# Eight PSUM banks as one pool instead of four pools, in a block-sparse attention and feed-forward kernel

## The chip, the cores and the metric

The kernel runs on one core of a Trainium2 chip. The metric is the device time of one execution in microseconds (us), the median of several runs; lower is better. The core has five engines that run their own instruction streams in order: the matrix engine (PE, whose weight loads are listed apart as PEld), the vector engine (DVE), the scalar engine (ACT), GpSimd (POOL) and the engine that only issues transfers (SP). PE writes its products into PSUM, an accumulation memory of eight banks, each 2 KB in each of 128 partitions; one product tile of 128x512 fp32 fills a bank. DVE and ACT read the banks and write to SBUF, the main on-chip memory.

## The reference

Four batches, eight heads, 768 positions, head size 64. Positions are grouped in 24 blocks of 32. A query block attends to itself and its two neighbours, to the first and the last block, and to three sampled blocks; the first and last query blocks attend to everything. The heads' outputs, side by side, are the input of a feed-forward layer with a swish that has a factor for each hidden column.

```python
scores = scale * np.matmul(q, k.transpose(0, 1, 3, 2))
mask = np.abs(blk_i - blk_j) <= window
mask = mask | (blk_i == 0) | (blk_j == 0) | (blk_i == n_blocks - 1) | (blk_j == n_blocks - 1)
for qb in range(n_blocks):
    for kb in sampled_blocks[qb]:
        mask[qb * block:(qb + 1) * block, kb * block:(kb + 1) * block] = True
scores = np.where(mask, scores, -1000000000.0)
scores = scores - np.max(scores, axis=-1, keepdims=True)
attn = np.exp(scores)
attn = attn / (np.sum(attn, axis=-1, keepdims=True) + 1e-09)
...
x = np.ascontiguousarray(attn_out.transpose(0, 2, 1, 3)).reshape(B * S, H * D)
...
h = x @ w_in
g = h * (1.0 / (1.0 + np.exp(-beta * h)))
return (g @ w_out).astype(np.float32)
```

`attn_out` is attn times v; x has 3072 rows of 512, h 2048 columns, and the result is 3072 x 512.

## The kernel before

**Attention.** Work goes in chunks of 128 query positions (4 blocks) of one batch, and each chunk in two quads Q of four heads: 4 x 6 x 2 = 48 steps. For each batch q, k and v are loaded and cast to fp16 (POOL after the start); q and k are transposed on PE into `qT` and `kT` (`transpose_pair`, PSUM tiles tp_q and tp_k, L209). `gather_chunk` copies the keys of each query block side by side into `KG` (ACT L250, POOL L255 and L261); the values come by DMA from a table in DRAM into `VA` and `VB` (`gather_v`, three buffers each).

One step consists of

- `scores`: 16 small products per pair of heads into two PSUM tiles sc (L321); DVE takes the negated maximum nm of each (L328) and ACT writes the exponentials probs (L331);
- `probs_T`: eight PE transposes of probs into one PSUM tile tp_p (L342), copied by DVE to probsT (L346);
- `attend`: products of probsT with VA and VB into one PSUM tile av (L393, and L405 for the global rows), whose last column is the row sum; DVE divides (L411, L412) and writes x16.

The rows of the first and last blocks are done once per batch and head pair in `global_scores` (two PSUM tiles scg, L358, read by DVE gnm L366 and twice by ACT gp L371) and `global_T` (PSUM tile tp_g, L380, copied by DVE to gpT, L383). When both quads of a chunk are done, `x_transpose` turns x16 on PE (tile tp_x, L435) into xT (DVE L437).

**Feed-forward.** Chunks are put together in groups of 2, 2, 4, 4, 4, 4, 4. For each group there are 16 units `h_unit`: four matmuls into a PSUM tile hps (L449), ACT tanh into t_sb (L453), DVE (t+1)*h into g (L455). For each chunk there are two half units `o_unit`: eight matmuls each into one PSUM tile ops (L466), which is held from the first half to the end of the second, then scaled by ACT into osb (L472) and stored. The units wait in a queue `moe_q` and `run_moe` deals them out between the attention pieces of the steps, to a plan by due times.

**Order.** `tc.manual_schedule(engines={ET.PE, ET.Pool, ET.SP})` keeps the instructions of PE, POOL and SP in the order in which the program traces them. DVE and ACT are ordered by a scheduler at build time. All engines run in order; semaphores are set by the framework. A tile of a PSUM pool with N buffers is given one of N banks, and its first matmul waits until the tile that had the bank before has been read for the last time.

**PSUM.** Four pools share the eight banks:

```python
sc_psum = ctx.enter_context(tc.tile_pool(name="sc_psum", bufs=2, space=bass.MemoryType.PSUM))
tp_psum = ctx.enter_context(tc.tile_pool(name="tp_psum", bufs=2, space=bass.MemoryType.PSUM))
av_psum = ctx.enter_context(tc.tile_pool(name="av_psum", bufs=1, space=bass.MemoryType.PSUM))
mm_psum = ctx.enter_context(tc.tile_pool(name="mm_psum", bufs=3, space=bass.MemoryType.PSUM))
```

sc and scg take the two banks of the first, all transposes (tp_k, tp_q, tp_p, tp_g, tp_x) the two of the second, av the one of the third, hps and ops the three of the last.

Of the kernel before, what the change touches and what calls it, by code (L numbers as in the profile page):

```python
# [10 lines left out]
FP32 = mybir.dt.float32  # L11
FP16 = mybir.dt.float16
# [8 lines left out]
def kernel(  # L21
# [43 lines left out]
    o_pool = ctx.enter_context(tc.tile_pool(name="osb", bufs=2))  # L65
    g_pool = ctx.enter_context(tc.tile_pool(name="gbuf", bufs=2))

    sc_psum = ctx.enter_context(tc.tile_pool(name="sc_psum", bufs=2, space=bass.MemoryType.PSUM))
    tp_psum = ctx.enter_context(tc.tile_pool(name="tp_psum", bufs=2, space=bass.MemoryType.PSUM))
    av_psum = ctx.enter_context(tc.tile_pool(name="av_psum", bufs=1, space=bass.MemoryType.PSUM))  # L70
    mm_psum = ctx.enter_context(tc.tile_pool(name="mm_psum", bufs=3, space=bass.MemoryType.PSUM))


    sb_handle = dataclasses.replace(sampled_blocks.tensor, shape=[NB, 6], dtype=I32)
# [129 lines left out]
    def transpose_pair(name, b, Q, pr):  # L204
        h16 = halves[(name, b, Q)]
        dstT = (qT if name == "q" else kT)[b]
        tp = tp_psum.tile([P, 1024], FP16, tag="tp", name=f"tp_{name}")
        for e in range(6):
            nc.tensor.transpose(out=tp[:, e * P:(e + 1) * P],  # L209
                                in_=h16[:, e, 2 * pr:2 * pr + 2, :].rearrange(  # L210
                                    "p h d -> p (h d)"),
                                identity=identity)
        return nc.scalar.activation(
            out=dstT[:, 2 * Q + pr, :].rearrange("p (s e) -> p s e", e=6),
            func=AF.Copy, scale=SCALE if name == "q" else 1.0,
            in_=tp[:, 0:S].rearrange("p (e s) -> p s e", e=6))
# [88 lines left out]
    def scores(b, c, Q, KG):  # L305
        scs = []
        for hp in range(2):
            sct = sc_psum.tile([P, 2, 256], FP32, tag="sc", name="sc")
            scs.append(sct)

        for hp in range(2):
            for pr in range(2):
                pg = 2 * Q + pr
                for j in range(4):
                    i = 4 * c + j
                    rr = slice(64 * hp, 64 * hp + 64)
                    if 0 < i < NB - 1:
                        rhs = KG[rr, j, pg, :]
                    else:
                        rhs = kT[b][rr, pg, 0:256]  # L320
                    nc.tensor.matmul(scs[hp][BLK * j:BLK * (j + 1), pr, :],  # L321
                                     lhsT=qT[b][rr, pg, i * BLK:(i + 1) * BLK],
                                     rhs=rhs, start=True, stop=True,
                                     tile_position=(64 * hp, BLK * j))
        pt = p_pool.tile([P, 4, 256], FP16, tag="probs", name="probs")
        nm = small_pool.tile([P, 2, 2], FP32, tag="nm", name="nm")
        for hp in range(2):
            nc.vector.tensor_reduce(out=nm[:, hp, :], in_=scs[hp], axis=AX.X, op=ALU.max,  # L328
                                    negate=True)
            for pr in range(2):  # L330
                last_exp[0] = nc.scalar.activation(  # L331
                    out=pt[:, 2 * pr + hp, :], in_=scs[hp][:, pr, :],
                    func=AF.Exp, bias=nm[:, hp, pr:pr + 1], scale=1.0)
        return pt
# [1 line left out]
    last_exp = [None]  # L336

    def probs_T(pt):
        tp = tp_psum.tile([P, 1024], FP16, tag="tp", name="tp_p")
        for u in range(4):  # L340
            for half in range(2):
                nc.tensor.transpose(out=tp[:, u * 256 + half * P:u * 256 + (half + 1) * P],  # L342
                                    in_=pt[:, u, half * P:(half + 1) * P],
                                    identity=identity)
        ptT = pt_pool.tile([P, 4, 2, P], FP16, tag="probsT", name="probsT")
        nc.vector.tensor_copy(out=ptT.rearrange("p u h q -> p (u h q)"), in_=tp)  # L346
        return ptT

    def global_scores(b, Q, hp):
        rr = slice(64 * hp, 64 * hp + 64)  # L350
        halves = []
        for s in range(2):
            sct = sc_psum.tile([P, 2, 256], FP32, tag="sc", name="scg")
            sct = sct.rearrange("p a w -> p (a w)")[:, 0:384]
            halves.append(sct)
            for j in range(4):
                pr, blk = j // 2, (j % 2) * (NB - 1)
                nc.tensor.matmul(sct[BLK * j:BLK * (j + 1), :],  # L358
                                 lhsT=qT[b][rr, 2 * Q + pr, blk * BLK:(blk + 1) * BLK],
                                 rhs=kT[b][rr, 2 * Q + pr, 384 * s:384 * (s + 1)],  # L360
                                 start=True, stop=True,
                                 tile_position=(64 * hp, BLK * j))
        nm = small_pool.tile([P, 4], FP32, tag="gnm", name="gnm")
        pg = gp_pool.tile([P, S], FP16, tag="gp", name="gp")
        for s in range(2):
            nc.vector.tensor_reduce(out=nm[:, s:s + 1], in_=halves[s],  # L366
                                    axis=AX.X, op=ALU.max, negate=True)
        nc.vector.tensor_reduce(out=nm[:, 2:3], in_=nm[:, 0:2], axis=AX.X, op=ALU.min)  # L368
        pv = pg.rearrange("p (e s) -> p e s", e=6)
        for s in range(2):  # L370
            nc.scalar.activation(  # L371
                out=pv[:, :, 64 * s:64 * (s + 1)],
                in_=halves[s].rearrange("p (s e) -> p e s", e=6),
                func=AF.Exp, bias=nm[:, 2:3], scale=1.0)
        return pg

    def global_T(pg):
        tp = tp_psum.tile([P, 1024], FP16, tag="tp", name="tp_g")
        for ct in range(6):
            nc.tensor.transpose(out=tp[:, ct * P:(ct + 1) * P],  # L380
                                in_=pg[:, ct * P:(ct + 1) * P], identity=identity)
        gT = gpt_pool.tile([P, 6, P], FP16, tag="gpT", name="gpT")
        nc.vector.tensor_copy(out=gT.rearrange("p c q -> p (c q)"), in_=tp[:, 0:S])  # L383
        return gT

    def attend(b, c, Q, ptT, VA, VB, gTs, x16):
        av = av_psum.tile([P, 4, VW], FP32, tag="av", name="av")
        js = [j for j in range(4) if 0 < 4 * c + j < NB - 1]
        for u in range(4):
            h = 4 * Q + u  # L390
            for half, V in ((0, VA), (1, VB)):
                for j in js:
                    nc.tensor.matmul(av[BLK * j:BLK * (j + 1), u, :],  # L393
                                     lhsT=ptT[:, u, half, BLK * j:BLK * (j + 1)],
                                     rhs=V[:, j, h * VW:(h + 1) * VW],
                                     start=(half == 0), stop=(half == 1),
                                     tile_position=(0, BLK * j))
        if len(js) < 4:
            j = 0 if c == 0 else 3
            bi = 0 if c == 0 else 1  # L400
            for u in range(4):
                pr, hp = u // 2, u % 2
                jj = 2 * pr + bi
                for ct in range(6):
                    nc.tensor.matmul(av[BLK * j:BLK * (j + 1), u, :],  # L405
                                     lhsT=gTs[hp][:, ct, BLK * jj:BLK * (jj + 1)],
                                     rhs=v16[b][:, ct, 4 * Q + u, :],
                                     start=(ct == 0), stop=(ct == 5),
                                     tile_position=(0, BLK * j))
        rec = small_pool.tile([P, 4], FP32, tag="rec", name="rec")  # L410
        nc.vector.reciprocal(out=rec, in_=av[:, :, D])  # L411
        nc.vector.tensor_tensor(out=x16[:, 4 * Q:4 * Q + 4, :], in0=av[:, :, 0:D],  # L412
                                in1=rec[:, :].to_broadcast([P, 4, D]), op=ALU.mult)
# [14 lines left out]
    def x_transpose(b, c, x16):  # L428
        gi, s = slot_of[(b, c)]
        if s == 0:  # L430
            xT_tiles[gi] = x_pool.tile([P, N_DMC, 512], FP16, tag="xT", name="xT")
        tp = tp_psum.tile([P, 1024], FP16, tag="tp", name="tp_x")
        xf = x16.rearrange("p h d -> p (h d)")
        for cc in range(N_DMC):
            nc.tensor.transpose(out=tp[:, cc * P:(cc + 1) * P],  # L435
# [7 lines left out]
    def h_unit(gi, f):  # L443
        n = P * len(groups[gi])
        if f == 0:
            g_tiles[gi] = g_pool.tile([P, N_FFC, 512], FP16, tag="g", name="g")
        hp = mm_psum.tile([P, 512], FP32, tag="mm", name="hps")
        for cc in range(N_DMC):
            nc.tensor.matmul(hp[:, 0:n], lhsT=w_in_sb[:, cc, f * P:(f + 1) * P],  # L449
                             rhs=xT_tiles[gi][:, cc, 0:n],  # L450
# [9 lines left out]

    def o_unit(gi, s, part):
        if part == 0:
            o_live[(gi, s)] = mm_psum.tile([P, D_MODEL], FP32, tag="mm", name="ops")
        op = o_live[(gi, s)]
        for f in range(8 * part, 8 * part + 8):
            nc.tensor.matmul(op, lhsT=g_tiles[gi][:, f, s * P:(s + 1) * P],  # L466
# [305 lines left out]
```

## Time and profile before

| | |
|---|---|
| time, median of three runs | 355.84 us (352.66 to 357.5) |
| profiled execution | 355.98 us |
| its span, first to last instruction | 354.1 us |
| mean granted PE clock | 0.96 of full |
| costliest lines of PE | L449 hps 101.2 us, L466 ops 89.9 us, L342 tp_p 33.5 us, L321 sc 29.3 us |
| costliest lines of DVE | L455 g 67.3 us, L328 nm 62.9 us, L346 probsT 32.5 us |
| costliest lines of ACT | L331 probs 76.8 us, L453 t_sb 69.6 us, L250 KG 34.0 us |

All times come from one profiled execution. Busy time counts an engine's instructions and not its waits; a wait is listed with the instruction that ended it. A page's slices divide the span into 40 parts of 8.9 us, and a digit is the busy share in tenths. A line such as `PE sc L321 <- ACT gp L371: 12.3, 10, 1.9` reads: PE, before an instruction of line 321 that writes sc, stood idle until ACT's instruction of line 371 that writes gp was done; 12.3 us in total, 10 times, the longest 1.9 us. In the timeline each row has its start, its length, and in brackets the idle time before it and what ended that.

### The profile page before, as it was taken

The page shows a single profiled execution, that of the slowest core. Times are in us where ns is not written, and L with a number is a line of the kernel's source. Part 1 is how long each engine was busy: PE and PEld are TensorE (multiplying, and loading weights), DVE is VectorE, ACT ScalarE, POOL GpSimd, SP SyncE. Part 2 cuts the span into 40 slices and gives each one's busy share as a digit, 9 for nine tenths or more (in the row PEclk, how much of TensorE's full clock was granted, in tenths as well). Part 3 has the DMA queues.
Part 4 walks back from the last instruction along what each step waited for, and adds up shares of the span by engine and source line. Part 5 has one row for each costly group of instructions (what it writes and reads, how often), then busy time and mean ns, then how long its engine had stood idle before and what let it go on. Part 6 is the DMA issues. An engine that isn't in the chain of part 4 may idle for free.

```text
span 354.1 us, 11302 instructions
## 1 busy us (share of the span) xinstructions
PE 299.5 (85%) x4288; PEld 168.8 (48%) x4288; DVE 227.1 (64%) x506; ACT 230.2 (65%) x447; POOL 174.3 (49%) x451
## 2 busy tenths in 40 slices
PE   0565877769687899986999999997889999899995
PEld 0343535646445565543545665453435655444442
DVE  3667766748778566678687668677777666543400
ACT  2687466988766888677678887666656664354421
POOL 5659939599957864955556819725015100000000
PEclk9999988989987889999899999999999999999999
DMA  7979999998887853655878617724036150000012
GB/s 182 380 202 223 225 323 314 291 227 184 200 291 226 246 149 84 169 138 142 254 221 245 168 35 190 184 69 103 33 88 156 43 141 31 31 30 31 31 71 79
DMA packets 40135, 56.95 MB, mean 161 GB/s; under 512 B 7280, under 2 KB 31984, under 8 KB 40080
## 3 DMA queue, kind: packets, MB, share of 16 engines
q0 software_dynamic: 10160, 26.21, 28.2%
q1 hardware_dynamic: 24400, 23.71, 25.5%
q10 hardware_dynamic: 5520, 6.30, 5.3%
q8 instruction: 34, 0.56, 0.7%
q14 instruction: 21, 0.17, 0.2%
HBM read 50.77 MB, written 9.62 MB: 171 GB/s over the span
## 4 chain that ended last, share of the span: by engine, by line
PE 56%; DVE 13%; ACT 13%; issue 5%; DMA 4%; POOL 2%; POOLq 0%; ACTq 0%; DVEq 0%; SPq 0%
PE ops L466 20%; PE hps L449 18%; ACT probs L331 5%; PE tp_p L342 5%; DVE g L455 4%; DMA VB<-vtab 4%; PE sc L321 3%; ACT gp L371 3%; DVE nm L328 3%; PE av L393 3%; ACT t_sb L453 3%; DVE gnm L366 2%; PE av L405 2%; ACT KG L250 2%; PE scg L358 1%
## 5 line engine op out<-in xcount | busy, mean ns | idle before, releaser
L449 PE MATMUL hps<-xT,w_in_sb 128*128 128x512 f16 (+1 forms) x448 | 101.2, 361 | 5.5 <-DVE g L455 4.9
L455 DVE SCALAR_TENSOR_TENSOR g<-t_sb,hps 128x512 f16<-128x512 f16 (+1 forms) x112 | 67.3, 609 | 49.5 <-ACT t_sb L453 48.3
L453 ACT ACTIVATE t_sb<-hps,beta_h_sb 128x512 f16<-128x512 f32 (+1 forms) x112 | 69.6, 634 | 39.2 <-PE hps L449 38.5
L466 PE MATMUL ops<-w_out_sb,g 128*128 128x512 f16 x384 | 89.9, 381 | 0.0
L331 ACT ACTIVATE probs<-sc,nm 128x256 f16<-128x256 f32 x192 | 76.8, 476 | 19.5 <-DVE nm L328 19.2
L328 DVE TENSOR_REDUCE nm<-sc 128x2 f32<-128x512 f32 x96 | 62.9, 686 | 26.7 <-PE sc L321 26.6
L280 POOL DMA_INDIRECT VB<-vtab,idx_b x40 | 38.9, 972 | 81.9 <-PE av L393 64.3
L261 POOL COPY KG<-kT 128x128 f16 (+1 forms) x264 | 63.2, 293 | 4.4 <-PE sc L321 4.0
L449 PEld LDWEIGHTS <-w_in_sb 128*128 128x128 f16 x448 | 43.0, 102 | 39.3 <-issue 9.2
L466 PEld LDWEIGHTS <-g 128*128 128x128 f16 x384 | 36.7, 98 | 43.2 <-issue 2.8
L321 PE MATMUL sc<-KG,qT 64*32 64x256 f16 x704 | 29.3, 292 | 13.7 <-ACT gp L371 9.0
L250 ACT COPY KG<-kT 128x768 f16<-128x768 f16 (+1 forms) x44 | 34.0, 782 | 6.5 <-PE sc L321 5.9
L342 PE MATMUL tp_p<-identity,probs 128*128 128x128 f16 x384 | 33.5, 236 | 1.2 <-issue 1.2
L346 DVE COPY probsT<-tp_p 128x1024 f16<-128x1024 f16 x48 | 32.5, 677 | 1.3 <-PE tp_p L342 1.1
L472 ACT ACTIVATE osb<-ops 128x512 f32<-128x512 f32 x24 | 14.4, 599 | 23.9 <-PE ops L466 23.9
L371 ACT ACTIVATE gp<-scg,gnm 128x384 f16<-128x384 f32 x32 | 16.8, 577 | 17.8 <-DVE gnm L368 13.3
L342 PEld LDWEIGHTS <-probs 128*128 128x128 f16 x384 | 24.2, 105 | 5.5 <-issue 3.1
L321 PEld LDWEIGHTS <-qT 64*32 64x32 f16 x768 | 9.6, 92 | 35.4 <-issue 24.0
L209 PE MATMUL tp_k<-identity,k 128*128 128x128 f16 x96 | 9.8, 252 | 14.2 <-ACT k L202 12.0
L393 PEld LDWEIGHTS <-probsT 128*32 128x32 f16 x1408 | 15.5, 99 | 12.4 <-issue 9.1
L412 DVE TENSOR_TENSOR x<-av,rec 128x256 f16<-128x256 f32 x48 | 20.2, 422 | 1.2
L393 PE MATMUL av<-VA,probsT 128*32 128x65 f16 x704 | 20.1, 201 | 0.9 <-DVE x L412 0.8
(69 smaller groups left out, 299.4 us busy)
## 6 DMA issues: line engine op xcount, KB each, us to landing
VA<-vtab SPq DMA_DIRECT2D x16, 390.0 KB
out_dram<-osb ACTq DMA_DIRECT2D x24, 256.0 KB
VB<-vtab SPq DMA_DIRECT2D x147, 32.5 KB
st_k<-in_k_dram POOLq DMA_DIRECT2D x6, 768.0 KB, 5.9
st_v<-in_v_dram POOLq DMA_DIRECT2D x6, 768.0 KB, 8.5
st_q<-in_q_dram POOLq DMA_DIRECT2D x6, 768.0 KB, 6.4
VA<-vtab SPq DMA_DIRECT2D x8, 292.5 KB
vtab<-v POOLq DMA_DIRECT2D x3, 780.0 KB, 7.1
```

Of the source, the lines that this page charges most:

```text
L250: (nc.scalar.copy if steady else nc.vector.tensor_copy)(out=KG[:, j0:j1, w0:w0 + 2, 0:96], in_=dataclasses.replace(base, ap=[ap[0], [BLK, ...
L261: eng.tensor_copy(out=KG[:, j, p0:p1, 128 + BLK * r:160 + BLK * r], in_=kv[:, p0:p1, bass.ds(k_regs[(4 * c + j, r)] * BLK, BLK)])
L280: nc.gpsimd.indirect_dma_start(VB[:, j, :], None, tab[:, :], bass.IndirectOffsetOnAxis(idx_b[:, 4 * c + j:4 * c + j + 1], 0))
L321: nc.tensor.matmul(scs[hp][BLK * j:BLK * (j + 1), pr, :], lhsT=qT[b][rr, pg, i * BLK:(i + 1) * BLK], rhs=rhs, start=True, stop=True, tile_ ...
L328: nc.vector.tensor_reduce(out=nm[:, hp, :], in_=scs[hp], axis=AX.X, op=ALU.max, negate=True)
L331: last_exp[0] = nc.scalar.activation(out=pt[:, 2 * pr + hp, :], in_=scs[hp][:, pr, :], func=AF.Exp, bias=nm[:, hp, pr:pr + 1], scale=1.0)
L342: nc.tensor.transpose(out=tp[:, u * 256 + half * P:u * 256 + (half + 1) * P], in_=pt[:, u, half * P:(half + 1) * P], identity=identity)
L393: nc.tensor.matmul(av[BLK * j:BLK * (j + 1), u, :], lhsT=ptT[:, u, half, BLK * j:BLK * (j + 1)], rhs=V[:, j, h * VW:(h + 1) * VW], start=( ...
L449: nc.tensor.matmul(hp[:, 0:n], lhsT=w_in_sb[:, cc, f * P:(f + 1) * P], rhs=xT_tiles[gi][:, cc, 0:n], start=(cc == 0), stop=(cc == N_DMC - 1))
L453: nc.scalar.activation(out=t_sb[:, 0:n], in_=hp[:, 0:n], func=AF.Tanh, bias=0.0, scale=beta_h_sb[:, f:f + 1])
L455: nc.vector.scalar_tensor_tensor(out=g_tiles[gi][:, f, 0:n], in0=t_sb[:, 0:n], scalar=1.0, in1=hp[:, 0:n], op0=ALU.add, op1=ALU.mult)
L466: nc.tensor.matmul(op, lhsT=g_tiles[gi][:, f, s * P:(s + 1) * P], rhs=w_out_sb[:, f, :], start=(f == 0), stop=(f == N_FFC - 1))
```

## The change

The four pools become one of eight banks, and every PSUM tile of the kernel is taken from it under one tag. Each tile is declared as a whole bank and then viewed in its former shape. No instruction is added or removed, and the traced order of the program stays.

```diff
-    sc_psum = ctx.enter_context(tc.tile_pool(name="sc_psum", bufs=2, space=bass.MemoryType.PSUM))
-    tp_psum = ctx.enter_context(tc.tile_pool(name="tp_psum", bufs=2, space=bass.MemoryType.PSUM))
-    av_psum = ctx.enter_context(tc.tile_pool(name="av_psum", bufs=1, space=bass.MemoryType.PSUM))
-    mm_psum = ctx.enter_context(tc.tile_pool(name="mm_psum", bufs=3, space=bass.MemoryType.PSUM))
+    ring = ctx.enter_context(tc.tile_pool(name="ring", bufs=8, space=bass.MemoryType.PSUM))
@@ transpose_pair; probs_T, global_T and x_transpose likewise
-        tp = tp_psum.tile([P, 1024], FP16, tag="tp", name=f"tp_{name}")
+        tp = ring.tile([P, 1024], FP16, tag="bank", name=f"tp_{name}")
@@ scores
-            sct = sc_psum.tile([P, 2, 256], FP32, tag="sc", name="sc")
+            sct = ring.tile([P, 512], FP32, tag="bank", name="sc").rearrange(
+                "p (a w) -> p a w", a=2)
@@ global_scores
-            sct = sc_psum.tile([P, 2, 256], FP32, tag="sc", name="scg")
-            sct = sct.rearrange("p a w -> p (a w)")[:, 0:384]
+            sct = ring.tile([P, 512], FP32, tag="bank", name="scg")[:, 0:384]
@@ attend
-        av = av_psum.tile([P, 4, VW], FP32, tag="av", name="av")
+        av = ring.tile([P, 512], FP32, tag="bank", name="av")[:, 0:4 * VW].rearrange(
+            "p (u e) -> p u e", e=VW)
@@ h_unit
-        hp = mm_psum.tile([P, 512], FP32, tag="mm", name="hps")
+        hp = ring.tile([P, 512], FP32, tag="bank", name="hps")
@@ o_unit
-            o_live[(gi, s)] = mm_psum.tile([P, D_MODEL], FP32, tag="mm", name="ops")
+            o_live[(gi, s)] = ring.tile([P, D_MODEL], FP32, tag="bank", name="ops")
```

More of the change, by code (lines that the diff above doesn't have):

```diff
@@ L338, in probs_T @@
     def probs_T(pt):
-        tp = tp_psum.tile([P, 1024], FP16, tag="tp", name="tp_p")
+        tp = ring.tile([P, 1024], FP16, tag="bank", name="tp_p")
         for u in range(4):
@@ L377, in global_T @@
     def global_T(pg):
-        tp = tp_psum.tile([P, 1024], FP16, tag="tp", name="tp_g")
+        tp = ring.tile([P, 1024], FP16, tag="bank", name="tp_g")
         for ct in range(6):
@@ L431, in x_transpose @@
             xT_tiles[gi] = x_pool.tile([P, N_DMC, 512], FP16, tag="xT", name="xT")
-        tp = tp_psum.tile([P, 1024], FP16, tag="tp", name="tp_x")
+        tp = ring.tile([P, 1024], FP16, tag="bank", name="tp_x")
         xf = x16.rearrange("p h d -> p (h d)")
```

## The prediction

> **What bounds the kernel now.** I read the page first: busy time, slices, chain of waits. Bounds of 2% (about what a measurement of this kernel can tell from no change) lie at 348.7 and 363.0 us around the median of 355.84.
>
> ```profile
> PE 299.5 (85%) x4288; PEld 168.8 (48%) x4288; DVE 227.1 (64%) x506; ACT 230.2 (65%) x447; POOL 174.3 (49%) x451
> ...
> PE   0565877769687899986999999997889999899995
> ...
> PEclk9999988989987889999899999999999999999999
> DMA  7979999998887853655878617724036150000012
> ...
> PE 56%; DVE 13%; ACT 13%; issue 5%; DMA 4%; POOL 2%; POOLq 0%; ACTq 0%; DVEq 0%; SPq 0%
> ```
>
> PE is the busiest engine and carries over half of the chain. It is idle for 54.6 us of 354.1; 16.0 of these fall before 28 us (loads, first casts), 3.7 after 310. The rest, some 35 us, is what a PSUM change can touch. The waits of the PE alone, from 28 us on, say who ended them:
>
> ```profile
> PE sc L321 <- ACT gp L371: 12.3, 10, 1.9
> PE hps L449 <- DVE g L455: 4.9, 4, 2.1
> PE scg L358 <- ACT probs L331: 3.0, 5, 0.8
> ...
> PE tp_k L209 <- DVE probsT L346: 2.2, 2, 1.3
> PE sc L321 <- ACT probs L331: 1.8, 1, 1.8
> ```
>
> (waiter, releaser, us in total, times, longest). None of these is a wait for data: a score product doesn't read gp, nor hps the g of the unit before. The releaser is the last reader of the bank that the waiter is about to overwrite. The timeline shows one such wait:
>
> ```profile
> 96.34 0.39 PE L435 MATMUL tp_x<-identity,x 128*128 128x128 f16 x4
> ...
> 97.63 1.05 ACT L371 ACTIVATE gp<-scg,gnm 128x384 f16<-128x384 f32 x2 [0.61 <-DVE gnm L368]
> 98.27 0.87 PE L321 MATMUL sc<-KG,qT 64*32 64x256 f16 x16 [1.53 <-ACT gp L371]
> ```
>
> PE ends tp_x at 96.73, then stands until ACT's first gp exponential has left a bank of the two-bank score pool; its KG had been ready for 9.7 us. I went through all 432 PSUM tiles this way, setting the first matmul of each against the end of the last reader of the tile before it in the same bank. 48 tiles after 28 us begin 0.05 us after that end, and the PE idle time before them is 29.0 us: 10.4 up to 84, 4.2 in 84-110, 4.3 in 110-150, 4.7 in 150-190, 0.2 in 190-230, 5.2 in 230-270, none later.
>
> **What the change moves.** It adds and removes no engine operation. In the built program the orders of PE, POOL and SP (with all DMA issues) are the same row for row; DVE and ACT are ordered by the scheduler, and 58 of 506 DVE rows and 62 of 446 ACT rows stand elsewhere, mostly one place away. The banks do not rotate strictly: of 424 reuses 177 come eight tiles later, 101 seven, 65 nine, 39 six; the nearest is four and the farthest 28, where an ops tile is held (up to 17.8 us).
>
> Are the new banks free in time? With the times of before, of all 424 reuses only one would come too early (scg at 107.7, by 0.18 us); the next tightest has 0.56 us left, nine have under 1 us, the median 3.2.
>
> **Term 1, waits after 84 us: 14.0 gained.** The ceiling is their 18.6 us. For a floor I leave all other engines where they are, and let each wait shrink only as far as the tightest data edge of the next 6 us allows (start of a matmul less the end of what it reads). That returns 3.3 of 4.2 in 84-110, 2.6 of 4.3, 4.1 of 4.7, 0.2 of 0.2 and 4.9 of 5.2: 15.2. The next waits are then those with the small margins: tp_p for probs (0.75 us at 219.7), tp_x for x16 (0.65 at 268.0), tp_k for POOL's cast (nothing at 115.6 and 186.8). Against it stand new bank waits: 0.2 us with the old times, 3.3 us (8 tiles) if PE always led its readers by 1 us, about the mean of the waits removed. I take 1.2, so 14.0; range 11.9 to 18.6. PE is in order, so behind such a wait all PE work queues, and DVE and ACT behind that.
>
> **Term 2, the clock: 2.5 gained.** PE's granted clock by stretch (PE busy, clock, DMA share, GB/s):
>
> ```profile
> 100.30:103.70 3.40, 3.40 (x23) 0.50 0.62 232
> 110.50:117.30 6.80, 6.05 (x86) 0.50 0.88 281
> 124.20:127.60 3.40, 3.40 (x74) 0.50 1.10 320
> 168.60:172.00 3.40, 3.40 (x19) 0.51 1.03 343
> ...
> 190.00:230.00 40.00, 39.49 (x627) 1.00 0.60 162
> ```
>
> Each slow stretch follows bank waits by a few us (96.7-98.3, 108.4-111.3, 121.1-123.7, 163.7-167.4). In one, the four hps matmuls of a unit take 1.71 us, against 0.86 elsewhere. 17.0 us at half clock cost up to 8.5 us; 240-270 has as many waits and no slow stretch, so the link is loose: I take under a third.
> The Trainium skill speaks against the change here (TensorE: Matmul & The Clock Gate, A second HAM failure mode: psum-queue depth-cycling): it tells of a kernel that cycled through PSUM banks each iteration, idled briefly between groups and so swung between half and full clock. By that rule the rate of 84-172 (five windows of 3.4 us in 88 us) would go on over 172-310, an estimate of 8 windows at 1.7 us, and the sum would be 356 instead of 340. Row 190:230, where three banks are cycled at clock 1.00, does not show it.
>
> **Term 3, waits before 84 us: 2.5 gained.** 10.4 us of bank waits, and a floor by data edges of 6.8, but others pace this stretch:
>
> ```profile
> 28.00:84.00 56.00, 41.16 (x818) 28.53 (x819) 38.54 (x92) 42.17 (x89) 45.40 (x114) 0.91 1.13 267
> ```
>
> (busy PE, PEld, DVE, ACT, POOL, clock, DMA share, GB/s). The DMA engines are over full, POOL is busy for 45.4 of 56 and hands PE the K and q casts and the KG gather of the second batch just in time. POOL itself waits for PE only once, 3.0 us for av L393 at 69.5. So 0 to 6.8; 2.5, near that row.
>
> **Term 4, the new DVE and ACT order: 2.5 lost.** A row moved ahead of one that was ready earlier delays it by a row's length (0.41 to 0.69 us). Taking each DVE row's input time from the old trace, rows stood behind a later-ready one for 22 us in total in the old order (after 40 us) and for 32 us in the new; ACT's went from 4 to 6. Of those 12 us the chain share of DVE and ACT, 26%, gives about 3; PE's earlier start hides some: 2.5, range 10 lost to 2.5 gained (the scheduler planned the new order for free banks). DVE is idle 36%; without that cover all 12 us would show.
>
> **Term 5, semaphores: 0.5 lost.** PE gets 15 more separate semaphore instructions (86 for 71); the trace has such a one at 51 ns: 0 to 0.8.
>
> Sum: 14.0 + 2.5 + 2.5 - 2.5 - 0.5 = 16.0. The profiled execution took 355.98 us (span 354.1 and 1.9 around it), 0.14 over the median: 355.98 - 16.0 = 340.0.
>
> **Rivals.**
> *The waits come back as data waits* (chance 0.16). For it: from 147 to 165 and 237 to 266 us the chain runs through DVE and ACT pieces (g, nm, probs, gp), and DVE is busy 16.4 of 20 us in 150-170. If these pace, only 110-150 (2.6) and 190-230 (0.2) come back, with the clock's 2.5 less terms 4 and 5: 2.3 gained, 353.7. Against: in those stretches DVE itself waits for sc and ACT, which a bank-blocked PE delivers late.
> *Slower: one late reader stops every kind of work* (0.10). Before, a late score reader blocked scores only; now the bank may be hps's or tp's. From 28 to 310 us a tile starts every 0.7 us, so eight tiles pass in 5.6 us; the longest holds are sc 5.0 and scg 4.5 us. If the new DVE/ACT order lengthens the hold of a score pair past that in each of the 36 steps from 84 us on, by 0.8 us, it costs 29 us: 340 + 29 = 369. It is slower by 2% from 0.64 us a step. Against: the moves of order are one place.
> *More than forecast* (0.06): all 18.6 us and all slow stretches (8.5) go, with term 3 and no losses: 29.6, so 326.4.
> *That the change doesn't do what it says*, a pool of eight in name only, is excluded by the bank list.
>
> The forecast has 0.68, its own range 330 to 348. Faster: 0.68 + 0.06 = 0.74; same 0.16; slower 0.10. The range 329 to 353 leaves out the fourth case, the slower one and a little of the second.
>
> **What would show it.** Right: in the waits of PE the rows sc <- gp, scg <- probs and hps <- g shrink from 20 us to under 5; PE idle in 84-270 falls from 19 to under 7 us; the end of the score products, now 293.7 us, comes some 15 us earlier; clock 0.50 stretches after 84 are fewer than five. Wrong: sc still waits for an ACT reader (the third case); tp_p, tp_g, tp_x wait for probs, gp, x16 for over 10 us (the second); before 84 us the gain exceeds 5 us (term 3); the clock falls below 1.00 after 172 us.

## The result, and the profile after

The changed kernel takes 339.04 us (median of 4 runs, 338.19 to 341.58), the kernel before 356.1 us beside it: a ratio of 0.9545, 95% interval 0.9494 to 0.9596. Ratios and their intervals, here and below, leave out runs more than 1.5% over the fastest of their kernel; medians are of all runs. The forecast was 340.0. The profiled execution took 339.05 us, its span 337.3.

The waits of PE alone in the changed kernel, from 28 us on (waiter, releaser, us in total, times, longest; lines 320 and 321, for instance, are the same statement, as the diff shifts the numbers):

```profile
PE tp_g L378 <- ACT gp L369: 6.7, 9, 2.2
PE tp_k L207 <- POOL k L200: 6.7, 2, 6.4
PE tp_x L434 <- DVE x L411: 4.2, 6, 1.4
PE tp_q L207 <- POOL q L200: 2.8, 2, 2.4
PE tp_p L341 <- issue: 2.2, 1, 2.2
```

The three rows of before are gone: sc no longer waits for gp, scg not for probs, and hps for g is 0.5 us. What is left are waits for data: tp_g reads gp, tp_k and tp_q the cast k and q, tp_x the x16. Matched tile by tile as in the prediction, the bank waits after 28 us fell from 29.1 to 1.5 us, and PE's other waits, nearly all for data, rose from 6.0 to 25.5 us. PE's idle time fell by only 7.1 us (54.6 to 47.5), but the span by 16.8. The other 9.7 us are busy time. The page's first line, its clock and the group of the score products:

```profile
PE 289.8 (86%) x4288; PEld 163.6 (49%) x4288; DVE 223.2 (66%) x506; ACT 226.7 (67%) x447; POOL 174.8 (52%) x451
...
PEclk9996997779997699998999999999999999999999
...
L320 PE MATMUL sc<-KG,qT 64*32 64x256 f16 x704 | 24.7, 291 | 6.2 <-DVE KG L259 3.2
```

and the same group in the kernel before:

```profile
L321 PE MATMUL sc<-KG,qT 64*32 64x256 f16 x704 | 29.3, 292 | 13.7 <-ACT gp L371 9.0
```

PE is busy for 9.7 us less with the same 4288 matmuls, 4.6 of them in the score products: these are busy for 24.7 us and were for 29.3, while one takes 291 ns and took 292. So they are not shorter, they lie closer together. The timeline of before showed the 16 products of a step (16 for all four heads, eight in each of the two sc tiles) at 98.27 lasting 0.87 us. The same step (the 16th) in the changed kernel:

```profile
91.15 0.39 PE L434 MATMUL tp_x<-identity,x 128*128 128x128 f16 x4
91.47 0.42 PE L320 MATMUL sc<-KG,qT 64*32 64x256 f16 x16
91.82 0.21 PE L392 MATMUL av<-VA,probsT 128*32 128x65 f16 x4
```

No wait stands before them, and the 16 last 0.42 us: the eight of one tile and the eight of the other, which use different row halves of the array, run at once. In the kernel before, the second tile's bank was released by the second gp exponential, 0.5 us after the first, and as PE was then working on the first tile, this second wait appears as busy time. In 13 of 45 steps after 28 us the second score tile began over 0.3 us after the first, and those pairs took 0.93 us on average against 0.45; after the change it is 1 of 44.

Stage by stage, from the 13th step (first of the second batch) to the 48th, in the changed kernel (window, length, busy PE, PEld, DVE, ACT, POOL, granted clock, DMA share, GB/s):

```profile
79.00:105.00 26.00, 23.12 (x463) 14.32 (x462) 23.31 (x59) 21.83 (x52) 20.10 (x51) 1.00 0.82 216
105.00:117.00 12.00, 5.76 (x42) 2.81 (x48) 2.31 (x7) 4.18 (x8) 10.13 (x25) 0.57 0.97 299
117.00:145.70 28.70, 28.70 (x530) 17.69 (x521) 22.49 (x46) 25.44 (x50) 20.33 (x54) 1.00 0.59 157
145.70:180.40 34.70, 32.98 (x502) 17.00 (x501) 28.41 (x61) 27.16 (x55) 25.03 (x60) 0.95 0.77 221
180.40:212.10 31.70, 31.42 (x539) 18.90 (x538) 22.85 (x45) 26.05 (x50) 20.40 (x54) 1.00 0.55 154
212.10:248.20 36.10, 35.51 (x507) 17.29 (x506) 28.57 (x60) 26.03 (x52) 12.21 (x36) 1.00 0.41 106
```

PE is 95 to 100% busy from 117 us on. The second line is a stall that the kernel before did not have: PE stands from 104.8 to 111.2 us before tp_k, until POOL has cast the third batch's keys, and its clock falls to half for 10.2 us around it. POOL in the changed kernel, then the same cast in the kernel before:

```profile
99.53 1.88 POOL L223 CAST v<-st_v 128x384 f16<-128x384 f32 x4 [4.06 <-DMA st_v<-in_v_dram]
110.23 1.85 POOL L200 CAST k<-st_k 128x384 f16<-128x384 f32 x4
```

```profile
114.22 1.85 POOL L202 CAST k<-st_k 128x384 f16<-128x384 f32 x4
```

PE is at tp_k 10.6 us earlier than before (104.8 against 115.4 us), the cast only 4.0 us earlier; POOL had itself stood for the load of v. The lead over the kernel before grows 4.0 us up to the 13th step, 7.7 at the 17th, falls to 6.0 at the 21st, after the stall, and then grows to 17.0 at the 45th.

### The profile page after: what moved, and what is told of

Its sections match the earlier page's. It is cut to its first block, busy times and chain, and to the rows that moved or that the text cites. A ratio compares the mean times of both kernels' runs of the same rounds, so it can differ in the third digit from the quotient of the medians.

```text
span 337.3 us, 11313 instructions
## 1 busy us (share of the span) xinstructions
PE 289.8 (86%) x4288; PEld 163.6 (49%) x4288; DVE 223.2 (66%) x506; ACT 226.7 (67%) x447; POOL 174.8 (52%) x451
## 3 DMA queue, kind: packets, MB, share of 16 engines
q0 software_dynamic: 10160, 26.21, 29.1%
## 4 chain that ended last, share of the span: by engine, by line
PE 59%; DVE 10%; ACT 8%; DMA 8%; issue 6%; POOL 6%; SPq 1%; POOLq 1%; DVEq 0%; ACTq 0%
PE ops L465 20%; PE hps L448 19%; PE tp_p L341 4%; DMA st_kq<-in_k_dram 4%; PE av L392 3%; PE sc L320 3%; DVE g L454 3%; ACT probs L330 3%; PE av L404 3%; DMA VA<-vtab 3%; DVE nm L327 2%; POOL KG L259 2%; ACT gp L369 2%; DVE gnm L364 2%; PE tp_k L207 2%
## 5 line engine op out<-in xcount | busy, mean ns | idle before, releaser
L448 PE MATMUL hps<-xT,w_in_sb 128*128 128x512 f16 (+1 forms) x448 | 98.7, 356 | 1.0 <-DVE xT L436 0.5
L465 PE MATMUL ops<-w_out_sb,g 128*128 128x512 f16 x384 | 90.9, 384 | 0.0
L448 PEld LDWEIGHTS <-w_in_sb 128*128 128x128 f16 x448 | 42.1, 100 | 34.0 <-issue 2.8
L341 PE MATMUL tp_p<-identity,probs 128*128 128x128 f16 x384 | 31.9, 229 | 2.8 <-issue 2.2
L320 PE MATMUL sc<-KG,qT 64*32 64x256 f16 x704 | 24.7, 291 | 6.2 <-DVE KG L259 3.2
L341 PEld LDWEIGHTS <-probs 128*128 128x128 f16 x384 | 23.2, 102 | 6.8 <-issue 3.7
L364 DVE TENSOR_REDUCE gnm<-scg 128x1 f32<-128x384 f32 x32 | 16.7, 550 | 8.6 <-PE scg L356 8.6
L392 PEld LDWEIGHTS <-probsT 128*32 128x32 f16 x1408 | 16.2, 99 | 11.8 <-issue 9.2
```

Source lines behind the costliest of these rows:

```text
L320: nc.tensor.matmul(scs[hp][BLK * j:BLK * (j + 1), pr, :], lhsT=qT[b][rr, pg, i * BLK:(i + 1) * BLK], rhs=rhs, start=True, stop=True, tile_ ...
L392: nc.tensor.matmul(av[BLK * j:BLK * (j + 1), u, :], lhsT=ptT[:, u, half, BLK * j:BLK * (j + 1)], rhs=V[:, j, h * VW:(h + 1) * VW], start=( ...
```

## The experiments

Theory A: the gain is the removed bank waits; a product finds a bank as soon as any is free. Rival B: the gain came from the new DVE and ACT order (the scheduler's). Rival C: the number of banks for a kind of product counts, sharing does little. In each run the kernel before is measured on the same chip.

**The same order on all engines, two bank plans.** Both kernels get, from step 4 on, the traced order on DVE and ACT as well:

```diff
+        if n == 4:
+            ctx.enter_context(tc.manual_schedule(
+                engines={ET.PE, ET.Pool, ET.SP, ET.DVE, ET.Activation}))
```

Four pools (e1):

> The four pools of before; from step 4 on DVE and ACT also keep the traced order (112 of 534 DVE and 109 of 474 ACT instructions move against before). Theory A (the gain is the bank waits): the bank waits stay, 25 to 35 us after 28 us, time 350 to 365. Rival B (the gain came from the new order that the scheduler found for DVE and ACT): nothing is said of this one alone, it is the base for e2.

One pool (e2):

> The pool of eight, with DVE and ACT in the same traced order as e1: all five engines have the same instructions in the same order in e1 and e2, so only the banks differ. Theory A: 13 to 20 us faster than e1, bank waits after 28 us under 4 us. Rival B: within 5 us of e1.

Measured: 385.7 us with four pools (ratio to before 1.0837, 1.0798 to 1.0875) and 357.07 with one (1.0033, 0.9997 to 1.0069): 28.6 us apart, more than theory A said, and the first one far above its range. Bank waits after 28 us are 47.6 and 15.0 us, where 25 to 35 and under 4 were expected. The longest waits of PE with four pools, then with one:

```profile
PE sc L321 <- ACT gp L371: 20.4, 12, 3.6
PE hps L449 <- DVE g L455: 8.8, 4, 3.4
```

```profile
PE tp_g L378 <- ACT gp L369: 7.0, 6, 2.0
PE tp_x L434 <- DVE x L411: 3.4, 6, 1.5
```

The banks alone make this difference, since nothing else differs; B falls as the cause of the gain as a whole. In the change itself the order of DVE and ACT moved too, and what that added or cost within the 17.1 us was not measured by itself. The size was off in part because more products were bank-blocked in the traced order (58 tiles over 47.6 us; 48 over 29.1 before). The clock differs too: its mean was 0.911 with four pools and 0.962 with one, and how much of the 28.6 us goes through it is not told apart. Order is not nothing: the traced one costs 30 us with four pools, and puts the one-pool kernel 18 us over the changed kernel.

**Fewer banks in one pool.**

```diff
-    ring = ctx.enter_context(tc.tile_pool(name="ring", bufs=8, space=bass.MemoryType.PSUM))
+    ring = ctx.enter_context(tc.tile_pool(name="ring", bufs=7, space=bass.MemoryType.PSUM))
```

> One pool of seven banks, the eighth unused; orders of DVE and ACT as in the changed kernel but for one instruction. Theory A (banks free in time because every product can take any free one): set against the recorded times of the changed kernel, 51 tiles would come too early, by 15 us in all, but against the times of before only 3; so some waits return: 341 to 346. Rival B: 338 to 340, as the order is the same. Rival C (the number of banks is what counts, sharing does little): over 347.

And with `bufs=6`:

> One pool of six banks, two unused. Theory A: 23 tiles come too early even with the times of before (7 us), so 344 to 352, still not slower than the four pools with eight banks. Rival C: over 356, since six banks are fewer than eight. Rival B: 338 to 341.

Measured: 342.48 us (0.9636, 0.9602 to 0.9669) with seven, 343.83 us (0.9659, 0.9610 to 0.9707) with six, just under its range. Bank waits after 28 us are 4.0 and 9.2 us. Six shared banks beat eight divided ones by 12 us; C falls, and both times are above what B said for them. The waits of PE with six banks:

```profile
PE tp_k L207 <- POOL k L200: 5.7, 2, 3.6
PE tp_q L207 <- POOL q L200: 5.1, 1, 5.1
PE tp_x L434 <- DVE x L411: 2.5, 4, 1.3
```

Data waits head the list here too: going from six to eight banks removes bank waits of 7.7 us, but brings 4.8 us to the end.

**Sharing in part.** Scores and feed-forward products in one pool of five, transposes and av as before; then scores, transposes and av in one pool of five, feed-forward as before:

```diff
+    ring = ctx.enter_context(tc.tile_pool(name="ring", bufs=5, space=bass.MemoryType.PSUM))
+    tp_psum = ctx.enter_context(tc.tile_pool(name="tp_psum", bufs=2, space=bass.MemoryType.PSUM))
+    av_psum = ctx.enter_context(tc.tile_pool(name="av_psum", bufs=1, space=bass.MemoryType.PSUM))
```

The first (e5):

> Scores and feed-forward products share five banks; the transposes keep their two, av its one. Theory A: the waits of sc and scg for each other and of hps for hps go (24 of the 29 us of before), those of the transposes stay (4.5 us): 341 to 346. Rival B (order): 31 ACT and 26 DVE instructions move against before, so no clear figure; equal to e6 only by chance.

The second (e6):

> Scores, transposes and av share five banks; feed-forward products keep their three. Theory A: sc, scg, transposes and av stop waiting (24 of 29 us), hps still waits for hps (5 us before, up to 7): 341 to 347.

Measured: 344.02 us (0.9682, 0.9606 to 0.9758) and 344.46 us (0.9628, 0.9534 to 0.9723), both in range. Either way of freeing the scores brings some 12 of the 17 us, though more bank waits are left than the 4.5 and the 5 to 7 us that were expected: 12.0 and 13.0 us.

**A third score bank, taken from the feed-forward.**

```diff
-    sc_psum = ctx.enter_context(tc.tile_pool(name="sc_psum", bufs=2, space=bass.MemoryType.PSUM))
+    sc_psum = ctx.enter_context(tc.tile_pool(name="sc_psum", bufs=3, space=bass.MemoryType.PSUM))
-    mm_psum = ctx.enter_context(tc.tile_pool(name="mm_psum", bufs=3, space=bass.MemoryType.PSUM))
+    mm_psum = ctx.enter_context(tc.tile_pool(name="mm_psum", bufs=2, space=bass.MemoryType.PSUM))
```

> Four pools as before, but three banks for the scores and two for the feed-forward products. Theory A: the score waits fall, but hps and ops have only two banks, one of them held by ops: with the times of before 51 us too early; time 365 to 395. If a third score bank were all that the change brings: 340 to 348.

Measured: 390.6 us (1.099, 1.090 to 1.108). PE's waits:

```profile
PE hps L449 <- DVE g L455: 35.3, 30, 2.2
PE ops L466 <- DVE g L455: 10.9, 13, 2.1
PE sc L321 <- ACT gp L371: 6.2, 6, 1.7
```

The score waits fell from 12.3 to 6.2 us, and the feed-forward, left with two banks of which ops holds one, waits 46 us. Of the two fixed divisions that were run neither comes near the shared pool; others were not tried.

**Strict rotation.** Seven banks given out in turn, ops in the eighth:

```diff
+    def nxt():
+        turn[0] += 1
+        return f"bank{turn[0] % 7}"
...
-        hp = ring.tile([P, 512], FP32, tag="bank", name="hps")
+        hp = ring.tile([P, 512], FP32, tag=nxt(), name="hps")
```

> Strict rotation: seven banks given out in turn in the program's order to everything but ops, which has the eighth for itself. Theory A: waits only where a reader is more than seven tiles late, 3 us with the times of before and up to 16 with those after: 340 to 346. Rival (one late reader stops every kind of work, the slower case of the prediction): over 356.

Measured: 346.12 us (0.9741, 0.9662 to 0.9820), just over its range and far under the rival's 356. Bank waits after 28 us are 7.8 us; 2.7 of them are ops waiting for ops in the last stage, which takes 64.0 us from the last scores to the end and 60.7 in the changed kernel. Here one late reader does not stop everything.

**Is the new data wait worth anything?** The third batch's k and q transposes one step later, in the changed kernel:

```diff
-        trs[o + 4] += [tr("k", 0, 0), tr("k", 0, 1)]
+        late = 1 if b == 2 else 0
+        trs[o + 4 + late] += [tr("k", 0, 0), tr("k", 0, 1)]
...
```

> The changed kernel with the eight k and q transposes of the third batch moved one step later each. In the changed kernel PE stands for 6.4 us at 104.8 to 111.2 us before tp_k until POOL has cast k. Theory W (this new data wait gives back part of the gain, because everything behind it on PE stands too): the 6.4 us mostly go and 3 to 5 us reach the end: 334 to 336. Rival Z (POOL and the loads pace this stretch, so PE waits for them at the next place, KG, VA or VB): 338 to 340, with the wait under another name.

And `global_T` later in the step, in the changed kernel and in the kernel before, and both edits together:

```diff
-        acts = [(0.2, do_GT)] if pend_G else []
+        acts = [(0.45, do_GT)] if pend_G else []
```

> The changed kernel with global_T (PE tile tp_g, which reads gp) at 0.45 of a step's feed-forward units in place of 0.2. tp_g waits for gp for 6.8 us in the changed kernel, 0.3 us in the kernel before. Theory W: these waits go; 2 to 5 us gained, 334 to 337. Rival Z: 338 to 341, the consumers of gT (av of the global rows) or other tiles wait in its place.

> The same edit of global_T in the kernel with four pools, where tp_g waits 0.3 us in all. Theory W: nothing to gain, 354 to 358; so an edit that pays in the one kernel and not in the other shows that the banks had hidden the data wait. If it gains as much here as in the changed kernel, the edit's worth has nothing to do with the pools.

> Both edits on the changed kernel. Theory W: the sum of both, 330 to 334. Rival Z: 337 to 340.

These four shared a chip on which the kernel before took 365.0 us, so only ratios are set against the others. Late k: 0.9326 (0.9252 to 0.9399), clear of the changed kernel's 0.9545 and its interval; the gap of 0.0219 times 356 us is 7.8 us, more than the 3 to 5 expected, but it sets ratios of two chips against each other. Late global_T: 0.9492 (0.9435 to 0.9549), not told apart from the changed kernel. The same in the kernel before: 1.0047 (1.0013 to 1.0081), no gain. Both: 0.9314 (0.9252 to 0.9377), as late k alone. The waits of PE with late k and with late global_T:

```profile
PE tp_g L378 <- ACT gp L369: 5.7, 8, 2.2
...
PE tp_k L207 <- POOL k L200: 2.4, 1, 2.4
```

```profile
PE sc L320 <- DVE KG L259: 6.2, 2, 5.9
PE tp_k L207 <- POOL k L200: 5.4, 2, 3.8
PE tp_g L378 <- ACT gp L369: 4.4, 6, 1.8
```

Late k leaves of the tp_k wait only one of 2.4 us, in the fourth batch at 180 us. Moving global_T takes 2.3 of 6.7 us off the tp_g wait, and the time does not show it; that question stays open. The changed kernel was not run on this chip. The like comparison on it is both edits against late global_T, which differ by late k alone: 341.82 us (337.99 to 351.02, seven runs) against 346.11 (344.44 to 348.82, six runs), 4.3 us less by medians and 6.5 by the ratios. The runs overlap but the ratios' intervals do not: late k gains, so rival Z fails, but how much is not settled, and the 3 to 5 us of theory W are possible. Late k has the lowest ratios of all versions, alone or with late global_T.

## Why the prediction was right

**Direction and mechanism.** The waits named as bank waits were bank waits, and the banks alone take most of them away (47.6 to 15.0 us from e1 to e2, where nothing else changes). Sum: 16.0 us forecast, 17.1 measured. That the two are so close is in part luck, as the terms show.

**Term 1 (14.0), with terms 4 and 5 and the clock.** From the 13th step to the 48th the kernel before took 210.5 us, the changed one 197.6: 12.9 us less, where terms 1, 2, 4 and 5 gave 13.5. The make-up was not as forecast, and two errors offset each other. Bank waits fell by 17.7 us there, but data waits rose by 11.3; the floor by data edges allowed for 3.4. The prediction had named the edge (tp_k has no margin at 115.6 us), but its floor looked only 6 us past each wait, and PE's leads add up: PE came to tp_k 10.6 us early and the key cast only 4.0 us, and 6.4 us were lost there in one block. So the first rival, that waits come back as data waits, happened to that extent. What made up for it is a cost that the idle time of before did not show: PE was busy 6.5 us less in this stretch, 4.0 of it in the score products that now overlap. The sign listed for this, PE idle in 84-270 under 7 us, failed: it is 12.5 us between the same steps. The sign listed for the first rival, tp_p, tp_g and tp_x waiting over 10 us for probs, gp and x16, appeared: tp_g and tp_x alone wait 10.9 us from 28 us on (6.7 and 4.2), 5.7 of them before the 13th step. The other signs of being right held: the three bank rows fell from 20 to 0.5 us, and the scores end 17 us earlier.

**New bank waits (1.2).** 0.9 us in that stretch; 1.5 us and 11 tiles from 28 us on.

**Term 2 (2.5).** Half-clock time after the 13th step went from 17.0 to 13.7 us, worth at most 1.7. Before the 13th step it grew from 10.2 to 17.1 us. So by these times the clock brought nothing overall; the sign of fewer than five windows was met only just (four windows of 3.4 us). The rule of the Trainium skill that was weighed against the change (TensorE: Matmul & The Clock Gate, A second HAM failure mode: psum-queue depth-cycling) did not show in the later part, where the estimate by it had eight windows at half clock: from 160.7 to 333 us, with all eight banks in use in turn, the granted clock is 1.00.

```profile
160.70:333.00 172.30, 169.24 (x2124) 87.30 (x2123) 107.03 (x214) 106.69 (x202) 54.34 (x140) 1.00 0.39 112
```

**Term 3 (2.5).** The 13th step begins at 79.0 us and began at 83.0: 4.0 us, inside the bounds of 0 to 6.8. Bank waits there fell by 9.9 us and other waits rose by 8.2, so others do pace the stretch, but not chiefly those that the prediction named: 4.1 of the 8.2 us are tp_g waiting for gp (ACT), 2.0 sc for a KG copy by DVE, 0.6 tp_q for POOL's q cast.

**Terms 4 and 5 (3.0 lost)** were not measured by themselves. From 28 us on DVE stood idle, with an instruction ready behind the one that it waited for, for 10.2 us in the changed kernel and 4.0 in the kernel before; ACT for 5.3 and 3.5. How much of it reached the end stays open.

**The slower rival.** The 5.0 us that the prediction set against the eight tiles' 5.6 were a hold at 13.7 us, before the stretch that the 5.6 are from. From 28 us on the longest holds grew from 3.8 to 4.6 us (sc) and from 4.5 to 4.9 (scg), all under 5.6, and the bank waits came to 1.5 us. Strict rotation over seven banks cost 7 us and not 29, and 3.3 of the 7 are in the last stage, where ops has a single bank.

## What to carry to other kernels

When PE waits for a tile that it does not read, the releaser is the bank's last reader; add those waits up by pool, and check with the recorded times whether a shared pool would have had a bank free. Six shared banks did better here than eight in four pools, and the one move of a bank from pool to pool that was tried lost 35 us. Then look at what PE reaches too early: the next gain was an operand that another engine had been preparing in time for the slower PE.

## What was not expected of the hardware

A wait can hide in busy time: score products of two tiles on different row halves of the array overlap when both banks are free (0.42 us for 16) and follow each other when one is late (0.87 us), with the same 0.29 us for one. A PE wait of 6.4 us came with 10.2 us at half clock; but short waits came with it as well: in the kernel before no wait of PE from 28 us on was longer than 2.1 us, and 27.3 us up to the last scores passed at half clock. And one chip of those used ran the kernel before in 365.0 us where the others took 356; there the kernel with late global_T waits once for 5.9 us at about 35 us before the first batch's scores, for a KG copy by DVE, a wait that took 1.8 us in the changed kernel's trace. Why that chip differs is not known.
